# A new order list for a fused linear-attention and gated feed-forward kernel

## The chip, the cores and the metric

The kernel runs on one core of one Trainium2 chip. The metric is the time of one execution in microseconds of the device (us); lower is better. A core has five engines that run side by side, each with its own queue of instructions that it takes strictly in the order written: TensorE (PE, matrix products; its weight loads are listed as PEld), VectorE (DVE), ScalarE (ACT), GpSimd (POOL) and SyncE (SP). An instruction waits for the semaphores of what it needs, and whatever stands behind it on the same engine waits with it. PE reads operands from the on-chip memory SBUF and writes sums to PSUM, which has eight banks here named 0 to 7. Copies between the chip's main memory and SBUF are made by 16 DMA engines; SP and POOL issue them. What POOL issues is listed as the software queue q0 (these loads also turn float32 into bfloat16), what SP issues as the hardware queue q1.

## What is computed

```python
def _attn_ref(q, k, v):                       # 4 batches, 8 heads, 768 positions, 64 per head
    gamma = 1.0 - 2.0 ** (-5.0 - np.arange(H))
    for t in range(S):
        state = gamma * state + np.einsum('bhd,bhe->bhde', k[:, :, t], v[:, :, t])
        y[:, :, t] = scale * np.einsum('bhd,bhde->bhe', q[:, :, t], state)
...
def _moe_ref(x, w_gate, w_val, w_out, rms_g): # x: 3072 rows of 512; 1536 hidden
    xn = x / np.sqrt(np.mean(x * x, axis=-1, keepdims=True) + 1e-06) * rms_g
    g = xn @ w_gate
    return g * (1.0 / (1.0 + np.exp(-g))) * (xn @ w_val) @ w_out
```

A decaying state per head is read by q, its result is normalised row by row, and a gated feed-forward layer follows.

## The kernel before

The 768 positions are cut into six chunks of 128, c = 0 to 5, and each chunk is worked for the four batches b = 0 to 3. The whole program is one string, `ORDER`: a list of some 1060 words. A loop at the end of the kernel takes word after word and calls the small function of that name, which issues its instructions at once. So the list sets the order of every engine's queue; nothing reorders it later. A word reads `name.arguments`, with `@D`, `@A`, `@P` or `@S` for the engine where there is a choice (DVE, ACT, POOL, SP) and `/n` for the PSUM banks. The words that matter here:

- `Lq`, `Lk`, `Lv` .c.b load q, k or v of a chunk and batch (L327, L329). On POOL they arrive as bfloat16; on SP they arrive as float32 in the tiles qf, kf and vf, and `Cq`, `Ck` and `V` turn them into the bfloat16 operands later. `tq` and `tk` are transposing DMAs on SP (L402), and `XE` on SP is another (L516).
- `wg`, `wv` and `wo` .n0.n1 load the weights' column groups n0 to n1 on POOL (L338, L345): w_gate and w_val have twelve groups of 128, loaded in five pieces each, w_out three pieces.
- `Tq`, `Tk` transpose q and k on PE (L381, L386); `A` is the q-k product of one chunk, for one or two batches (L418), with 64 rows of the array used by each matmul; `M0`, `M1` mask it; `Y` forms the result of a chunk (L456, L460).
- `K` is the state product k times v (L541): eight matmuls that each use 64 columns of the array. `U` adds it to the running state and `B` makes the bfloat16 copy that the next chunk's `Y` reads. `P` is `A` and a part of `Y` for two batches together.
- `S`, `R`, `N`, `X`/`XE` are the row normalisation, its reciprocal root on POOL and the transposed copy xnT.
- `g` and `v` .c.n0.n1.b0.b1 are the two products of the feed-forward layer into PSUM (L564), `s` is the activation and `h` the product hT. The last chunk's are done with seven products in place of eight (`ga1` to `vc3`, L750, with sums `gS`, `vS`, `X1` to `X4` of operands).
- `a1`, `a6`, `a7`, `a4`, `b2`, `c5`, `c3` .c.r0.r1 are the seven products of hT and w_out that replace eight (L660), over sums `z1` to `z4` and `w1` to `w4`; `q` keeps a partial sum, `r1` to `r4` form the four quarters of a chunk's result and `s1` to `s4` .c store them (L688). A fourth argument of `a4`, `c3`, `r` and `s` means one half of a quarter.
- `H` and `hot` are matmuls on ones that nobody reads.

A DMA issued from SP uses one of eight completion slots in turn (DMAHW0 to 7), and one from POOL another eight (DMASW0 to 7); the ninth waits until the first has landed. One more rule stands in the load function:

```python
        if c == 2:
            after(i, ("wo", 8))
```

so that the loads of chunk 2 wait until the w_out piece `wo.8.12` has landed. Loads of other chunks have no such line; they wait only for a free buffer (four each of qf and kf, six of vf), for their completion slot, and for what stands ahead of them on their engine.

Of the kernel before, what the change touches and what calls it, by code (L numbers as in the profile page):

```python
# [17 lines left out]
Lk.0.2@S H.8/0 Lk.1.1@S rms.1@S yt ident iota pick Lk.0.0@P Ck.0.2@D Lq.0.1@P Tk.0.2/1 vd Lq.0.0@P mk1 H.3/2 D.0.2@D  # L18
Lk.0.1@P mk0 Lq.0.2@P Lk.0.3@P Lq.0.3@P Tk.0.0/3 Lv.0.0@P H.1/4 Ek.0.0@D Tq.0.1/5 hot.3/6 Lv.0.1@P J.0.0/7 Eq.0.1@A
Tq.0.0/0 D.0.0@D Lv.0.2@P Eq.0.0@A Tk.0.1/2 Ek.0.2@D H.1/4 Ek.0.1@A Tq.0.2/3 Lv.0.3@P yd hot.2/6 A.0.0/5710 Eq.0.2@D  # L20
tab wg.0.2 G/4 M0.0.0 wv.0.2 M1.0.0 Tq.0.3/2 GE@A wg.2.4 M0.0.1 Tk.0.3/6 Eq.0.3@A Y.0.0/3 M1.0.1 Lq.1.1@P A.0.2/57
Ek.0.3@A H.3/4 M1.0.2 S.0.0 A.0.3/12 M0.0.2 R.0.0 H.1/0 M1.0.3 Y.0.2/6 wv.2.4 K.0.0/4 N.0.0 S.0.2 J.0.1/7 Y.0.1/0
H.1/5 M0.0.3 R.0.2 S.0.1 X.0.0/2 J.0.3/3 U.0.0@A XE.0.0@D H.2/5 R.0.1 Ck.1.1@A N.0.2 Y.0.3/1 g.0.0.2.0.1/4 B.0.0 S.0.3
N.0.1 K.0.2/2 X.0.2/5 s.0.0.2.0.1 wg.4.6 v.0.0.2.0.1/6 U.0.2@A XE.0.2@D X.0.1/4 D.0.1@D R.0.3 v.0.0.2.2.3/0 XE.0.1@A
h.0.0.2.0.1 g.0.0.2.2.3/2 wv.4.6 D.0.3@D g.0.0.2.1.2/5 s.0.0.2.2.3 g.0.2.3.0.3/7 causal h.0.0.2.2.3 s.0.0.2.1.2
Lk.1.2@P N.0.3 g.0.3.4.0.3/6 D.1.1@D v.0.0.2.1.2/4 Lk.1.0@P s.0.3.4.0.3 K.0.1/3 s.0.2.3.0.3 h.0.0.2.1.2 X.0.3/2
Tk.1.1/5 mc.0@P U.0.1@A XE.0.3@A Lk.1.3@P g.0.0.4.3.4/0 g.0.4.6.3.4/1 wg.9.12 s.0.0.4.3.4 J.0.2/6 K.0.3/4 Lq.1.2@P
v.0.0.4.3.4/7 Lq.1.3@P v.0.4.6.3.4/3 h.0.0.4.3.4 v.0.2.3.0.3/2 mc.1@P s.0.4.6.3.4 v.0.3.4.0.3/0 U.0.3@A h.0.2.3.0.3
Tk.1.2/6 h.0.4.6.3.4 Lq.1.0@P g.0.5.6.0.3/7 Ek.1.2@D h.0.3.4.0.3 Tq.1.1/1 wv.9.12 s.0.5.6.0.3 g.0.4.5.0.3/4 Eq.1.1@D
wg.6.9 v.0.4.5.0.3/2 Ek.1.1@D s.0.4.5.0.3 Tk.1.0/3 Lv.1.3@P v.0.5.6.0.3/6 Ek.1.0@A g.0.9.10.0.4/0 Lv.1.0@P h.0.5.6.0.3  # L30
h.0.4.5.0.3 Tq.1.3/7 s.0.9.10.0.4 Tk.1.3/1 Lv.1.1@P Eq.1.3@D Tq.1.2/5 Ek.1.3@A Tq.1.0/4 Eq.1.2@D g.0.11.12.0.4/3
Lv.1.2@P Eq.1.0@D A.1.3/62 D.1.0@P s.0.11.12.0.4 g.0.10.11.0.4/0 M0.1.3 M1.1.3 A.1.2/71 wv.6.9 s.0.10.11.0.4
# [12 lines left out]
Cq.2.1@D g.1.2.3.0.3/6 w4@D tk.2.2 B.1.0 g.1.7.8.0.4/7 s.1.2.3.0.3 h.1.9.10.0.4 g.1.10.11.0.4/4 tq.2.3 h.1.2.3.0.3
s.1.4.5.0.4 v.1.5.6.0.4/0 z3.0.2@D z1.1.0@P s.1.7.8.0.4 h.1.4.5.0.4 tk.2.1 v.1.10.11.0.4/6 Cq.2.0@D s.1.10.11.0.4
z3.1.0@P h.1.5.6.0.4 a1.0.0.3/2 Lv.2.2@S h.1.10.11.0.4 tk.2.0 z2.0.2@P v.1.7.8.0.4/5 q1.0@A tq.2.0 V.2.3@A z4.0.2@P
A.2.2/1734 h.1.7.8.0.4 b2.0.0.3/0 M0.2.3 tq.2.1 z1.1.1@P M1.2.3 a6.0.0.3 V.2.0@P M1.2.2 Lv.2.1@S r1.0 Lk.3.3@S V.2.2@P
M0.2.2 Y.2.3/6 Lv.3.3@S q6.0@D S.2.3 A.2.0/5347 Lq.3.1@S R.2.3 a1.1.0.3/0 M0.2.1 M0.2.0 V.2.1@P Lq.3.3@S Y.2.2/1
M1.2.0 a7.0.0.3 z2.1.1@P S.2.2 M1.2.1 N.2.3 Lk.3.2@S R.2.2 Y.2.0/4 z1.1.2@D q7.0@A Y.2.1/5 S.2.0 N.2.2 XE.2.3@S  # L50
K.2.1/3 c5.0.0.3/7 S.2.1 R.2.0 U.2.1@D XE.2.2@S R.2.1 N.2.0 K.2.0/6 a4.0.0.3 z2.1.0@P N.2.1 XE.2.0@S r2.0 K.2.3/1
r4.0@A b2.1.0.3/3 U.2.0@D XE.2.1@S z2.1.2@D q1.1@A U.2.3@D z4.1.2@P Ck.3.3@A z3.1.2@D c3.0.0.3 Lq.3.2@S z4.1.0@P
Lq.3.0@S V.3.3@D K.2.2/4 Lk.3.0@S a6.1.0.3 U.2.2@D B.2.3 r3.0 Lv.3.2@S B.2.1 K.3.3/5 g.2.10.11.0.4/6 Cq.3.3@P U.3.3@D
r1.1 g.2.4.5.0.4/2 s.2.10.11.0.4 Cq.3.1@P tq.3.3 Ck.3.2@A v.2.4.5.0.4/1 s.2.4.5.0.4 B.2.0 tk.3.2 g.2.11.12.0.4/4
h.2.4.5.0.4 B.2.2 z3.1.1@D g.2.5.6.0.4/7 tk.3.3 Cq.3.2@D g.2.2.3.0.4/5 tq.3.2 v.2.10.11.0.4/3 s.2.2.3.0.4 s.2.5.6.0.4
v.2.5.6.0.4/6 Lk.3.1@S h.2.10.11.0.4 Lv.3.1@S Cq.3.0@D v.2.2.3.0.4/2 s.2.11.12.0.4 tq.3.1 Ck.3.0@D g.2.6.7.0.4/1
# [762 lines left out]
```

## Time and profile before

| what | value |
|---|---|
| time, median of 3 runs (lowest to highest) | 230.48 us (230.33 to 231.29) |
| span of the profiled execution, first to last instruction | 228.9 us |
| PE busy | 219.0 us, 96% of the span |
| DVE busy | 179.8 us, 79% |
| POOL busy | 162.5 us, 71% |
| ACT busy | 98.1 us, 43% |
| granted TensorE clock | full in all 40 slices |
| DMA moved | 33.64 MB, mean 147 GB/s |

The runs' times and the profiled execution's span differ by 1.58 us at the median, which lies outside the first and last instruction; the profile gives no other time of its own. The page cuts the span into 40 slices of 5.7 us and gives a busy digit in tenths for each. A group's row gives line, engine, operation and tiles, how many, busy time and mean. The timeline gives start, length and operation; matmuls overlap, so the distance from one start to the next is what a group took, not its length.

### The profile page before, as it was taken

What the parts mean: (1) busy time and instruction counts of PE and PEld (TensorE: products, weight loads), DVE (VectorE), ACT (ScalarE), POOL (GpSimd) and SP (SyncE); (2) the same over time, 40 slices, a digit from 0 to 9 for tenths busy, and PEclk for the clock granted to TensorE, in tenths of its full rate; (3) what the DMA queues carried; (4) which work ended last, traced back from release to release, by engine and by line L of the source; (5) the groups of instructions that cost most, each with busy time, mean ns of one, the idle gap of its engine ahead of it and who ended that gap; (6) DMA issues with size and microseconds to landing.
All of it is one profiled execution on the core that took longest, in us unless ns stands there. A gap on an engine that the chain in (4) does not pass through costs nothing.

```text
span 228.9 us, 5499 instructions
## 1 busy us (share of the span) xinstructions
PE 219.0 (96%) x2119; PEld 145.6 (64%) x2119; DVE 179.8 (79%) x325; ACT 98.1 (43%) x218; POOL 162.5 (71%) x214
## 2 busy tenths in 40 slices
PE   7799989999999999999999999999999999999991
PEld 2568744675447886446574448674457788888871
DVE  6599359889999968679747878791997789999850
ACT  7776342533247252362602424514335328754311
POOL 8979999658998979514584997886198899330800
PEclk9999999999999999999999999999999999999999
DMA  7999999999456888777989579469974432000254
GB/s 134 162 183 131 143 169 177 205 199 241 109 117 138 195 155 171 127 164 172 194 206 204 122 135 259 93 150 226 195 157 157 77 102 92 3 0 3 76 186 153
DMA packets 108171, 33.64 MB, mean 147 GB/s; under 512 B 94449, under 2 KB 108145, under 8 KB 108146
## 3 DMA queue, kind: packets, MB, share of 16 engines
q1 hardware_dynamic: 84674, 25.70, 49.8%
q0 software_dynamic: 23472, 7.60, 30.6%
q8 instruction: 16, 0.26, 0.4%
q14 instruction: 9, 0.07, 0.2%
HBM read 28.31 MB, written 6.29 MB: 151 GB/s over the span
## 4 chain that ended last, share of the span: by engine, by line
PE 59%; ACT 0%; DVE 0%; issue 0%
PE g_ps L564 14%; PE v_ps L564 14%; PE a L660 10%; PE c L660 6%; PE b L660 2%; PE ga L750 2%; PE va L750 2%; PE a_ps L418 1%; PE vc L750 1%; PE gc L750 1%; PE y_ps L456 1%; PE y_ps L460 1%; PE kv_ps L541 1%; PE vb L750 1%; PE gb L750 1%; ACT r L152 0%
## 5 line engine op out<-in xcount | busy, mean ns | idle before, releaser
L574 ACT ACTIVATE sg<-g_ps 128x512 bf16<-128x512 f32 (+2 forms) x64 | 35.9, 570 | 71.1 <-PE g_ps L564 63.2
L564 PE MATMUL g_ps<-xnT,wg_b 128*128 128x512 bf16 (+2 forms) x296 | 58.7, 339 | 0.9 <-ACT xnT L152 0.5
L564 PE MATMUL v_ps<-xnT,wv_b 128*128 128x512 bf16 (+2 forms) x296 | 59.2, 339 | 0.0
L586 DVE TENSOR_TENSOR hT<-sg,v_ps 128x512 bf16<-128x512 bf16 (+2 forms) x64 | 40.1, 647 | 18.7 <-PE v_ps L564 17.5
L564 PEld LDWEIGHTS <-wg_b 128*128 128x128 bf16 x296 | 25.3, 98 | 23.4 <-DMA wg_b<-in_moe_w_gate_dram 0.8
L564 PEld LDWEIGHTS <-wv_b 128*128 128x128 bf16 x296 | 25.6, 98 | 22.3
L660 PEld LDWEIGHTS <-hT 128*128 128x128 bf16 x288 | 27.6, 98 | 4.7
L633 POOL TENSOR_TENSOR z<-hT,z 128x512 bf16<-128x512 bf16 x14 | 16.9, 1218 | 12.7 <-PE a L660 6.7
L660 PEld LDWEIGHTS <-z 128*128 128x128 bf16 x216 | 20.8, 98 | 3.6 <-issue 0.7
L497 DVE SCALAR_TENSOR_TENSOR xn<-y_ps,rstd,g_bc 128x512 bf16<-128x512 f32 x22 | 16.5, 749 | 6.7 <-POOL rstd L485 6.5
L556 POOL CAST st_b<-st_f 64x256 bf16<-64x256 f32 x40 | 20.5, 513 | 1.4
L441 DVE TENSOR_TENSOR am<-a_ps,causal 128x512 bf16<-128x512 f32 x32 | 20.1, 680 | 1.6 <-PE a_ps L418 1.4
L473 ACT ACTIVATE xsq<-y_ps 128x512 bf16<-128x512 f32 x22 | 13.2, 600 | 16.1 <-PE y_ps L460 11.8
L660 PE MATMUL a<-wo_b,hT 128*128 128x256 bf16 x144 | 17.9, 273 | 0.0
L633 POOL TENSOR_TENSOR z<-z,hT 128x512 bf16<-128x512 bf16 x8 | 10.2, 1273 | 7.4 <-DVE z L633 3.8
L485 POOL TENSOR_TENSOR rstd<-ms,mhalf 128x1 f32<-128x1 f32 x24 | 13.7, 570 | 2.0
L483 POOL TENSOR_SCALAR ms<-ssq 128x1 f32<-128x1 f32 x24 | 4.7, 197 | 11.5 <-ACT xsq L473 10.3
L633 POOL TENSOR_TENSOR z<-hT 128x512 bf16<-128x512 bf16 x9 | 10.7, 1190 | 3.0 <-DVE hT L586 2.9
L683 DVE TENSOR_TENSOR r<-c,sn 128x512 f32<-128x512 f32 (+1 forms) x13 | 8.4, 645 | 5.5 <-PE c L660 4.4
L152 ACT COPY sn<-a 128x512 f32<-128x512 f32 x14 | 8.2, 583 | 10.5 <-PE a L660 10.5
L373 POOL TENSOR_TENSOR vp<-vf,vdec 128x512 bf16<-128x512 f32 x11 | 11.5, 1058 | 0.7 <-DMA vf<-in_v_dram 0.7
L441 DVE TENSOR_TENSOR am<-a_ps,mask 128x512 bf16<-128x512 f32 x16 | 10.1, 683 | 0.2 <-PE a_ps L418 0.2
(158 smaller groups left out, 396.0 us busy)
## 6 DMA issues: line engine op xcount, KB each, us to landing
out_dram<-r SPq DMA_DIRECT2D x22, 256.0 KB, 2.4
kf<-in_k_dram SPq DMA_DIRECT2D x18, 256.0 KB, 4.1
qf<-in_q_dram SPq DMA_DIRECT2D x16, 256.0 KB, 3.9
vf<-in_v_dram SPq DMA_DIRECT2D x16, 256.0 KB, 3.7
wo_b<-in_moe_w_out_dram POOLq DMA_DIRECT2D x3, 512.0 KB, 10.0
qb<-in_q_dram POOLq DMA_DIRECT2D x8, 128.0 KB, 5.6
vp<-in_v_dram POOLq DMA_DIRECT2D x8, 128.0 KB, 7.3
kb<-in_k_dram POOLq DMA_DIRECT2D x6, 128.0 KB, 5.1
```

Source lines behind the costliest of these rows:

```text
L373: e.tensor_tensor(out=u["vp"], in0=u["vf"], in1=vdec[:, c, :, None].to_broadcast([128, H, D]), op=ALU.mult)
L441: DVE.tensor_tensor(out=u["am"][:, i], in0=u["a"][i], in1=m, op=ALU.mult)
L473: ACT.activation(xsq, flat(u["y"]), AF.Square, accum_out=u["ssq"])
L485: POOL.tensor_tensor(out=u["rstd"], in0=ms, in1=mhalf, op=ALU.pow)
L497: DVE.scalar_tensor_tensor(out=u["xn"], in0=flat(u["y"]), scalar=u["rstd"], in1=g_bc, op0=ALU.mult, op1=ALU.mult)
L556: POOL.tensor_copy(st_b[b][r, :, i * 64:i * 64 + 64], st_f[b][r])
L564: nc.tensor.matmul(p[:, (n - n0) * m:(n - n0 + 1) * m], W[w][0][:, s, n * 128:(n + 1) * 128], xnT[c][:, s, b0 * C:b1 * C], start=s == 0, s ...
L574: ACT.activation(sg[:, :cols], done["wg", c, n0, b0][:, :cols], AF.Silu)
L586: DVE.tensor_tensor(out=h_of(c, r)[:, i:i + n1 - n0, b0 * C:b1 * C], in0=sg, in1=p, op=ALU.mult)
L633: e.tensor_tensor(out=x, in0=a, in1=b, op=how)
L660: nc.tensor.matmul(done[x, c][:, q], left(i, c, r)[:, k, q * C:q * C + C], right(i)[:, r, k], start=first and q == r == k == 0, stop=r == ...
L750: nc.tensor.matmul(p[:, q], l[:, r, q], m[:, k], start=first and q == k == 0, stop=q == k == 1, skip_group_check=True)
```

## The change

The change is a new string `ORDER`; no other line differs. The same operations are called as before, except that the words `a4.4.0.3`, `r4.4` and `s4.4` (the last quarter of chunk 4) are each split into two halves. Some elementwise operations are given to another engine (about ninety words change their letter, as many towards DVE as away from it), and the banks differ. On PE the state products `K` now stand next to each other or next to an `A`: counted along PE's queue, the 41 groups of `A`, `K`, `P` and of transposes onto half the array stood in 39 separate places before and stand in 22 now. Of the weights, `wv.2.4` is now issued before `wg.2.4` and `wg.4.6` before the first load of chunk 1 on POOL; `wo.8.12` now stands ahead of `wg.6.9` and `wv.6.9`. The word `yd` (an exponential on ACT) moves behind the first activations.

```diff
-Lk.0.2@S H.8/0 Lk.1.1@S rms.1@S yt ident iota pick Lk.0.0@P Ck.0.2@D Lq.0.1@P Tk.0.2/1 vd Lq.0.0@P mk1 H.3/2 D.0.2@D
...
+H.1/0 rms.1@S Lq.0.2@P H.3/1 Lk.0.0@P Lk.0.2@S Lq.0.0@P yt Lk.0.1@P Lq.0.1@P H.2/2 iota H.8/3 H.3/4 H.1/5 Lk.0.3@P
...
```

The head of SP's queue before, with what each row waits for (kf, qf and vf are loads of k, q and v):

```order
L329 DMA kf<-in_k_dram 128x8x64 x2
L306 DMA g_row<-in_moe_rms_g_dram 1x512
L329 DMA qf<-in_q_dram 128x8x64 [waits DMASW1_49]
L329 DMA kf<-in_k_dram 128x8x64 x2
L329 DMA qf<-in_q_dram 128x8x64
```

and now, up to the first load of chunk 2, the row that waits for DMASW4:

```order
L306 DMA g_row<-in_moe_rms_g_dram 1x512
L329 DMA kf<-in_k_dram 128x8x64 x2
L329 DMA qf<-in_q_dram 128x8x64
L329 DMA vf<-in_v_dram 128x8x64 x3
L329 DMA kf<-in_k_dram 128x8x64
L329 DMA qf<-in_q_dram 128x8x64 [waits DMAHW0_49]
L329 DMA kf<-in_k_dram 128x8x64 [waits DMAHW1_49]
L329 DMA kf<-in_k_dram 128x8x64 [waits DMAHW2_49,Activation_49]
L329 DMA qf<-in_q_dram 128x8x64 [waits DMAHW3_49]
L329 DMA vf<-in_v_dram 128x8x64 [waits DMAHW4_49]
L402 DMA_TRANSPOSE kT<-kb 128x4x128 [waits DVE_49,DMAHW5_49,PE_49,Activation_49]
L329 DMA kf<-in_k_dram 128x8x64 [waits DMAHW6_49,DVE_49]
L329 DMA kf<-in_k_dram 128x8x64 [waits DMAHW1_49,DMAHW7_49,DMASW4_49,DVE_49]
```

Before, two loads were issued and then came a load of chunk 2 (the qf row that waits for DMASW1, the slot of `wo.8.12`). Now twelve loads stand ahead of the first transpose, ten of them of chunks 3 and 4.

POOL's queue before, from the piece `wv.9.12` on:

```order
L338 DMA wv_b<-in_moe_w_val_dram 128x4x384
L338 DMA wg_b<-in_moe_w_gate_dram 128x4x384
L329 DMA vp<-in_v_dram 128x8x64 x4
L532 TENSOR_TENSOR kd<-kb,vdec 128x512
L338 DMA wv_b<-in_moe_w_val_dram 128x4x384
L345 DMA wo_b<-in_moe_w_out_dram 128x4x512
```

and now, from the same piece:

```order
L338 DMA wv_b<-in_moe_w_val_dram 128x4x384
L297 TENSOR_TENSOR mask_102<-causal,vdec 128x512
L345 DMA wo_b<-in_moe_w_out_dram 128x4x512
L556 CAST st_b_128<-st_f_124 64x4x64 x2
L556 CAST st_b_126<-st_f_122 64x4x64 x2
L329 DMA vp<-in_v_dram 128x8x64
L338 DMA wg_b<-in_moe_w_gate_dram 128x4x384
L338 DMA wv_b<-in_moe_w_val_dram 128x4x384
```

The last two of the twelve column groups' pieces, `wg.6.9` and `wv.6.9`, now come behind a piece of w_out of 512 KB, which is `wo.8.12`.

PE's queue in chunk 2 before, one row for each new product (kv_ps is a state product, and each row stands for the matmuls of its product):

```order
L541 MATMUL kv_ps_1678<-vp_1597,kb_1353 64x64
L660 MATMUL c_1687<-w1_1254,z_985 128x256
L541 MATMUL kv_ps_1715<-vp_1521,kb_1348 64x64
L660 MATMUL a_1428<-w4_1380,hT_588 128x256
L541 MATMUL kv_ps_1743<-vp_1457,kb_1307 64x64
L660 MATMUL b_1754<-wo_b_135,hT_1246 128x256
```

and now:

```order
L660 MATMUL a_1488<-wo_b_135,hT_627 128x256
L541 MATMUL kv_ps_1665<-vp_1278,kb_1303 64x64
L541 MATMUL kv_ps_1694<-vp_1376,kb_1301 64x64
L541 MATMUL kv_ps_1711<-vp_1625,kb_1238 64x64
L541 MATMUL kv_ps_1730<-vp_1550,kb_1188 64x64
L564 MATMUL v_ps_1739<-xnT_1041,wv_b_134 128x512
```

The four state products of a chunk, each between two full-array products before, now follow one another.

More of the change, by code (lines that the diff above doesn't have):

```diff
@@ L23 @@
[L23 to L32, printed above, removed]
@@ L103 @@
-c3.5.2.3.1 r3.5.1 c3.5.2.3.0 r3.5.0 s4.5.1@S s4.5.0@S s3.5.0@S s3.5.1@S b2.5.2.3 r1.5 s1.5@S z4.4.1@P c3.4.0.3 r3.4
-s3.4@S a4.4.0.3 r4.4@A s4.4@S
+H.1/0 rms.1@S Lq.0.2@P H.3/1 Lk.0.0@P Lk.0.2@S Lq.0.0@P yt Lk.0.1@P Lq.0.1@P H.2/2 iota H.8/3 H.3/4 H.1/5 Lk.0.3@P
+ident mk0 H.1/6 Lv.0.2@P H.1/7 Lv.0.0@P Ck.0.2@A G/0 Tk.0.2/1 pick Tq.0.2/2 Ek.0.2@D vd D.0.2@D Lq.0.3@P Tk.0.0/3 mk1
+Eq.0.2@A causal A.0.2/45 Lv.0.1@P Ek.0.0@D Tq.0.0/6 Eq.0.0@A Tk.0.1/7 Ek.0.1@A wg.0.2 Lv.0.3@P J.0.0/1 Tq.0.1/2 tab
```

158 lines of the change are left out of this document (84 added, 74 removed).

## The prediction

> **What bounds the kernel now.** I read the page first, then the waits of PE, the chain of waits, the timeline of the start, and last the DMA's rates by stretch. On the page:
>
> ```profile
> span 228.9 us, 5499 instructions
> PE 219.0 (96%) x2119; PEld 145.6 (64%) x2119; DVE 179.8 (79%) x325; ACT 98.1 (43%) x218; POOL 162.5 (71%) x214
> PE   7799989999999999999999999999999999999991
> DMA  7999999999456888777989579469974432000254
> ```
>
> PE is busy in all but the ends. In the first ten slices, up to 57 us, the DMA engines are as full as PE. The waits of PE, those of the first 90 us and then the one late wait:
>
> ```profile
> PE t_ps L381 <- DMA kb<-in_k_dram: 1.3, 1, 1.3
> PE g_ps L564 <- DMA wg_b<-in_moe_w_gate_dram: 0.4, 1, 0.4
> PE kv_ps L541 <- DVE vp L373: 0.4, 1, 0.4
> ...
> PE c L660 <- DVE r L683: 0.5, 1, 0.5
> ```
>
> So from about 35 us on PE runs through, with 0.9 us of waits, and the end is set by when PE gets its last weights and by its work from there. Up to that point the loads pace it: the wait of 0.4 us is for a weight piece. I therefore count from the first use of the last piece of w_val, `wv.6.9`, by the word `v.0.8.9`; about the same PE work stands ahead of it in both orders. Its issue on POOL, the time such a piece takes to land, and its first use on PE:
>
> ```profile
> 35.36 0.82 POOL L338 DMA_DIRECT2D wv_b<-in_moe_w_val_dram  x1
> ...
> wv_b<-in_moe_w_val_dram POOLq DMA_DIRECT2D x2, 384.0 KB, 7.5
> ...
> 45.22 1.03 PE L564 MATMUL v_ps<-xnT,wv_b 128*128 128x512 bf16 x4
> ```
>
> It lands at about 35.36 + 7.5 = 42.9 and is used at 45.22: the order has 2.3 us to spare there, no more.
>
> **Loads on SP: the term that decides.** Before, SP issues two loads of k at the start and then stands still:
>
> ```profile
> 0.79 1.06 SPq L329 DMA_DIRECT2D kf<-in_k_dram  x2
> ...
> SPq L329 <- DMA wo_b<-in_moe_w_out_dram: 46.1, 1, 46.1
> ```
>
> It waits 46.1 us for `wo.8.12`, because the next row is a load of chunk 2. In the new order ten loads of chunks 3 and 4 stand ahead of that row. The first seven loads wait for nothing and the next five for landings of early ones and for one cast on ACT. So the chip issues them in the first microseconds, wherever the list has them, and they meet the loads that PE needs. The DMA's rate by stretch (the last three columns are the granted clock, the mean share of a DMA engine and GB/s):
>
> ```profile
> 3.40:3.90 0.50, 0.50 (x3) 0.15 (x1) 0.50 (x3) 0.50 (x3) 0.50 (x2) 1.00 1.24 281
> 3.80:48.80 45.00, 41.82 (x582) 27.01 (x580) 33.81 (x59) 25.04 (x62) 39.46 (x62) 1.00 1.55 170
> 41.00:48.00 7.00, 7.00 (x83) 4.21 (x80) 5.80 (x10) 4.72 (x12) 4.47 (x10) 1.00 1.25 206
> 50.50:58.50 8.00, 8.00 (x65) 4.42 (x62) 7.73 (x13) 2.56 (x5) 6.83 (x7) 1.00 1.08 245
> ```
>
> From 3.8 to 48.8 only POOL's queue moves data, and the engines' share stays above one: packets queue up all that time. From 50.5 to 58.5 only SP's loads move, at 245 GB/s and a share of 1.08, which is full too. At 3.4 to 3.9 both queues are at work, and the share (1.24) is no higher than for one alone (1.25 in 41 to 48). The two queues divide one capacity. A load on SP is 262,144 bytes: 1.07 us at 245 GB/s, 0.93 us at 281. Ten of them take 9.3 to 10.7 us of all 16 engines. The price for the piece `wv.6.9` lies between 0, if POOL's queue were served first, and 10.7 us, if all ten are through before it. I take 9.3, from the row in which both queues run. It needs no even division: what SP's queue is given in the first 45 us is lost to POOL's, and at a quarter of the engines all ten would be through by then. At one seventh, the 40 us of POOL's loads from 3.8 to the landing of `wv.6.9` would still take 40 x 7/6 = 46.7, 6.7 us more.
>
> On this the Trainium skill, DMA: Bandwidth & Descriptors, section "Queues, rings and completion order", says that a DMA engine goes round the queue rows that have work and drains one packet from each in turn. By that rule SP's loads get their turns from the start, and the sum stays as it is; the trace has only the half microsecond of 3.4 to 3.9 with both at work.
>
> Behind these loads on SP stand transposes and the loads of chunk 2; on POOL, the reciprocal roots of chunk 0's normalisation stand behind weight loads that wait for one of eight slots to land. Both come late by the same wait for data, so I don't count them again.
>
> **Order of the weights.** `wo.8.12`, 512 KB, now stands ahead of `wv.6.9`, so its landing moves by 524,288 bytes at 206 GB/s, 2.5 us, to 45.4. Without any crowding `v.0.8.9` would start at about 45.5, 0.3 us later than before; the slack covers the rest. The pieces issued sooner are early ones, and what sets the later pace is the last. `wo.8.12` is also the gate of chunk 2: when it has landed, up to five loads of chunk 2 join `wg.6.9` and `wv.6.9` on the engines, which costs from 0 to 5 x 1.07 = 5.4 us. Before SP comes to them it has a transpose that waits for a cast, and most of `wg.6.9` is moved by then; I take 0.5.
>
> **State products side by side.** The price of a change between full-array products and half-array ones, from the chain (start, length, what):
>
> ```profile
> 105.27 0.24 PE kv_ps L541 x8
> 105.52 1.42 PE a L660 x12
> ...
> 116.67 1.31 PE a L660 x12
> ```
>
> and from the timeline of the start, two transposes onto half the array that follow one another:
>
> ```profile
> 11.80 0.44 PE L381 MATMUL t_ps<-pick,qb 128*64 128x64 bf16 x16
> 12.07 0.42 PE L381 MATMUL t_ps<-pick,kb 128*64 128x64 bf16 x16
> ```
>
> A state product of eight matmuls takes 0.24 us, and makes the product behind it 0.11 longer (1.42 against 1.31): 0.35. Sixteen such matmuls among their like take 0.27 (11.80 to 12.07), eight 0.135. The change of mode costs 0.21 us, there and back. The places of half-array work fall from 39 to 22; behind `v.0.8.9` from 23 to 11. Twelve fewer are 2.5 us. All of this is on PE's own path, with no cover; the five ahead of `v.0.8.9` save nothing, since PE waits for loads there. The bounds are 0 and 3.6 us (all 17).
>
> The skill's page TensorEngine Tiling (Array Packing), section "Key Properties", says that changing the mode drains the array while changing only the tile does not. By it, the two merges of a state product with a q-k product save only half each, 0.2 us less in all; no row here has such a pair.
>
> **The end.** The last rows on the way out, and the landing of stores of 256 and 128 KB:
>
> ```profile
> 220.35 0.42 DVE L683 TENSOR_TENSOR r<-c,sn 128x256 f32<-128x256 f32 x1 [1.38 <-PE c L660]
> ...
> 224.30 0.58 ACT L152 COPY r<-a 128x512 f32<-128x512 f32 x1 [3.80 <-PE a L660]
> ...
> out_dram<-r SPq DMA_DIRECT2D x22, 256.0 KB, 2.4
> ...
> out_dram<-r SPq DMA_DIRECT2D x4, 128.0 KB, 1.7
> ```
>
> PE ends at 224.27 (before the row at 224.30), and 4.63 us follow. The last piece is now half a quarter: 0.42 in place of 0.58, and 1.7 in place of 2.4, so 0.85 less, 3.8. The other half of chunk 4's quarter lies between the halves of `c3.5`, which covers the wait of 0.5 us for DVE's r. The stores before it could still be under way: 0 to 0.85.
>
> **Other moves.** `yd` behind the activations brings two more table loads on ACT:
>
> ```profile
> L302 ACT ACT_TABLE_LOAD x1 | 1.3, 1283 | 0.0
> ```
>
> Twice 1.28 us, while ACT is 43% busy, and behind it wait an activation and a copy of chunk 0's xnT. The late weights hide it; uncovered it could cost up to 2.6. Some ninety elementwise words change engine. DVE and POOL at 79% and 71% have room, but a single word can come late: the rows of 0.4 and 0.5 us above are such cases. I drop those two waits (0.9) and put 0.5 in, with 0 to 1.5 as bounds.
>
> **The sum**, against the profiled execution: `v.0.8.9` at 45.5 + 9.3 + 0.5 = 55.3. From there to PE's end before: 224.27 - 45.22 = 179.05; less 2.5, less 0.9, plus 0.5 is 176.15. PE ends at 231.45; plus 3.8 is a span of 235.25. The runs lie 1.58 above the span (230.48 against 228.9): **236.8 us**.
>
> **The rivals.**
> - *No crowding: faster.* POOL's queue keeps its rate and SP's loads fill gaps. Then 45.5 + 176.15 + 3.8 + 1.58 = **227.0 us**. For it: the mean of 170 GB/s against 206 leaves some gaps, and the two queues overlap for half a microsecond only. Against it: a share above one through 45 us. It decides if SP's ten loads cost POOL's queue under 2.5 us.
> - *Half the crowding: no change.* If SP's loads get a tenth of the engines or finish partly in gaps, 4 to 5 us are lost, and the savings of 3.5 to 4 us cancel them: 227.0 + 4.5 = **231.5**.
> - *Both crowdings: slower still.* The loads of chunk 2 go ahead of `wg.6.9` and `wv.6.9` too: 236.8 + 4.9 = **241.7**. For it: these are the last pieces, with 2.3 us to spare before. Against it: the transpose ahead of them on SP.
> - *The savings fail.* Neighbouring state products cost as before: 236.8 + 2.5 = 239.3, inside the forecast's range.
>
> **Chances.** The forecast with its own range, 233 to 240: 0.62. No crowding 0.20, half of it 0.08, both 0.10. Differences under 0.5% (1.15 us) can't be told from no change in this kernel. Faster by more: 0.20; within: 0.05; slower: 0.75, which has the rest of the half case. For eight in ten the range goes from 226.5 to 241.
>
> **What would show it.** Right: on SP twelve loads issued within the first 15 us; POOL's landings late by some 9 us at 45; PE idle before 57 us, on loads of q, k, v and weights, for about 10 us more than before; `v.0.8.9` near 55; from there on the same chain, shorter by 2.5 us; four state products of chunk 2 in about 0.65 us plus 0.1. Wrong: if the weights land as before and PE starts `v.0.8.9` before 47, the crowding is not there. If PE waits late for DVE or POOL by more than 1.5 us, the exchange of engines matters more than I said.

## The result and the profile after

| | before | after |
|---|---|---|
| time, median (lowest to highest) | 230.78 us (230.33 to 231.29) | 262.44 us (261.31 to 262.76) |
| ratio with 95% interval | | 1.1388 (1.1329 to 1.1448) |
| span of the profiled execution | 228.9 us | 259.6 us |

The change costs 31.7 us; the forecast was 6.3, and its whole range, up to 241, lies below the result. The page of the changed kernel, with its row of the clock:

```profile
PE 225.8 (87%) x2097; PEld 150.1 (58%) x2119; DVE 188.5 (73%) x324; ACT 96.6 (37%) x204; POOL 163.9 (63%) x218
...
PE   8837759976179799999989999999999979999894
...
PEclk9977988999759979999999999999999999999999
```

PE falls to a tenth of a slice where slices were full before, and the clock, which was full throughout, drops there and just behind to as little as a half. The DMA's rows by queue from 4 to 47 us (packets, MB, share of 16 engines), before:

```profile
q0 software_dynamic: 22946, 7.09, 155.6%
...
q1 hardware_dynamic: 179, 0.04, 0.5%
```

and after:

```profile
q0 software_dynamic: 18465, 4.76, 109.8%
q1 hardware_dynamic: 11439, 2.88, 46.6%
```

The sum hardly moves (7.13 and 7.64 MB). Of the 2.88 MB that SP's queue got, POOL's queue lost 2.33. SP's timeline after, and then PE, POOL and ACT around the forecast's mark:

```profile
2.29 0.99 SPq L329 DMA_DIRECT2D qf<-in_q_dram  x1
3.32 6.65 SPq L329 DMA_DIRECT2D vf<-in_v_dram  x3
...
27.21 4.02 SPq L329 DMA_DIRECT2D vf<-in_v_dram  x1
45.87 1.29 SPq L402 DMA_TRANSPOSE kT<-kb  x1
47.26 6.08 SPq L329 DMA_DIRECT2D kf<-in_k_dram  x3
```

```profile
62.40 1.04 PE L564 MATMUL v_ps<-xnT,wv_b 128*128 128x512 bf16 x4 [1.79 <-DMA wv_b<-in_moe_w_val_dram]
...
69.83 0.42 PE L541 MATMUL kv_ps<-vp,kd 128*64 128x64 bf16 x8 [4.08 <-ACT sg L574]
...
72.58 0.61 PE L510 MATMUL xt_ps<-ident,xn 128*128 128x128 bf16 x4 [2.32 <-DVE xn L497]
```

```profile
69.78 1.03 POOL L354 TENSOR_TENSOR qb<-qf,ydec 128x512 bf16<-128x512 f32 x1 [10.86 <-DMA qf<-in_q_dram]
70.90 0.19 POOL L483 TENSOR_SCALAR ms<-ssq 128x1 f32<-128x1 f32 x1
```

```profile
68.67 0.62 ACT L152 CAST kb<-kf 128x512 bf16<-128x512 f32 x1 [6.50 <-DMA kf<-in_k_dram]
```

`v.0.8.9` starts at 62.40 in place of 45.22. Behind it POOL stands 10.86 us on the cast `Cq.2.3`, whose load of q has not landed, with the reciprocal root `R.1.1` queued behind. ACT stands 6.50 us on the cast `Ck.2.0`, with an activation behind. PE waits 4.08 us for that activation and 2.32 for the xn that the root releases, and runs at half clock there (from 68 to 77 us). In the list before, `Cq.2.3` had 19 us of PE work between `v.0.8.9` and itself; in the new one it has 0.9. The waits of PE from 110 us on are these; all but the second lie behind 190 us, in the new end, and sum to 3.4:

```profile
PE a L660 <- DVE hT L633: 1.8, 1, 1.8
PE y_ps L460 <- POOL st_b L556: 0.9, 1, 0.9
PE a L660 <- DVE sn L152: 0.7, 1, 0.7
PE a L660 <- DVE vf L762: 0.4, 1, 0.4
PE a L660 <- ACT sn L152: 0.3, 1, 0.3
PE vb L750 <- DVE vf L762: 0.2, 1, 0.2
```

Before, there was one wait of 0.5 in all that time. Two of the forecast's small terms hold. The four state products of chunk 2 take 0.63 us from start to start, and the last rows on PE end at 256.05, 3.55 us before the span's end:

```profile
106.24 0.69 PE L541 MATMUL kv_ps<-vp,kb 128*64 128x64 bf16 x32
106.87 1.04 PE L564 MATMUL v_ps<-xnT,wv_b 128*128 128x512 bf16 x3
...
255.67 0.38 PE L660 MATMUL c<-wo_b,z 128*128 128x256 bf16 x2
```

### The profile page after: what moved, and what is told of

It reads as the page before. It is cut to its first block, busy times and chain, and to the rows that moved or that the text cites. A ratio compares the mean times of both kernels' runs of the same rounds, so it can differ in the third digit from the quotient of the medians.

```text
span 259.6 us, 5453 instructions
## 1 busy us (share of the span) xinstructions
PE 225.8 (87%) x2097; PEld 150.1 (58%) x2119; DVE 188.5 (73%) x324; ACT 96.6 (37%) x204; POOL 163.9 (63%) x218
## 3 DMA queue, kind: packets, MB, share of 16 engines
q1 hardware_dynamic: 84690, 25.70, 46.2%
## 4 chain that ended last, share of the span: by engine, by line
PE 38%; DVE 8%; POOL 7%; DMA 4%; issue 1%; SPq 1%; ACT 0%; POOLq 0%; DVEq 0%
PE v_ps L564 9%; PE g_ps L564 9%; PE a L660 8%; PE c L660 4%; DMA qf<-in_q_dram 4%; DVE hT L586 4%; DVE vf L762 2%; POOL vp L373 2%; POOL z L633 2%; PE b L660 2%; POOL st_b L556 1%; PE ga L750 1%; PE y_ps L460 1%; PE va L750 1%; PE y_ps L456 1%
## 5 line engine op out<-in xcount | busy, mean ns | idle before, releaser
L564 PE MATMUL v_ps<-xnT,wv_b 128*128 128x512 bf16 (+2 forms) x284 | 63.3, 355 | 6.5 <-DMA wv_b<-in_moe_w_val_dram 3.6
L564 PE MATMUL g_ps<-xnT,wg_b 128*128 128x512 bf16 (+2 forms) x286 | 61.0, 348 | 1.9 <-DMA wg_b<-in_moe_w_gate_dram 1.1
L586 DVE TENSOR_TENSOR hT<-sg,v_ps 128x512 bf16<-128x512 bf16 (+2 forms) x64 | 40.4, 646 | 20.3 <-ACT sg L574 11.9
L564 PEld LDWEIGHTS <-wv_b 128*128 128x128 bf16 x296 | 27.2, 103 | 30.0 <-issue 5.8
L564 PEld LDWEIGHTS <-wg_b 128*128 128x128 bf16 x296 | 27.0, 102 | 24.3 <-issue 2.0
L633 POOL TENSOR_TENSOR z<-hT 128x512 bf16<-128x512 bf16 x12 | 14.4, 1201 | 16.0 <-DVE hT L586 15.8
L354 POOL TENSOR_TENSOR qb<-qf,ydec 128x512 bf16<-128x512 f32 x9 | 10.2, 1132 | 18.5 <-DMA qf<-in_q_dram 17.6
L633 POOL TENSOR_TENSOR z<-hT,z 128x512 bf16<-128x512 bf16 x11 | 14.6, 1331 | 4.7 <-DVE z L633 4.4
L373 POOL TENSOR_TENSOR vp<-vf,vdec 128x512 bf16<-128x512 f32 x13 | 13.8, 1069 | 0.2
L633 POOL TENSOR_TENSOR z<-z,hT 128x512 bf16<-128x512 bf16 x11 | 13.0, 1185 | 0.8 <-DVE z L633 0.6
L456 PE MATMUL y_ps<-vp,am 128*128 128x64 bf16 x176 | 8.9, 195 | 4.6 <-DMA vp<-in_v_dram 4.5
```

The source lines that it names most:

```text
L373: e.tensor_tensor(out=u["vp"], in0=u["vf"], in1=vdec[:, c, :, None].to_broadcast([128, H, D]), op=ALU.mult)
L456: nc.tensor.matmul(y[:, h, :], u["am"][:, h % 2, h // 2, :], u["vp"][:, h, :], start=h == 0, stop=c == 0 and h == H - 1, skip_group_check= ...
L564: nc.tensor.matmul(p[:, (n - n0) * m:(n - n0 + 1) * m], W[w][0][:, s, n * 128:(n + 1) * 128], xnT[c][:, s, b0 * C:b1 * C], start=s == 0, s ...
L586: DVE.tensor_tensor(out=h_of(c, r)[:, i:i + n1 - n0, b0 * C:b1 * C], in0=sg, in1=p, op=ALU.mult)
L633: e.tensor_tensor(out=x, in0=a, in1=b, op=how)
```

## The experiments

### Early loads alone, in the order before

Ten and five extra loads on SP, with nothing else changed:

```diff
+    def early(e, bk, n):
+        for i in range(n):
+            x = ring([128, H, D], F32, *(("qf", 4) if i < 4 else ("vf", 6)))
+            SP.dma_start(out=x, in_=rows["k"][i % B, 3 + i // B])
...
-rms.1@S yt
+rms.1@S early.10 yt
```

> The order before, with ten more loads on SP's queue behind its first three: 256 KB each, k of chunks 3 to 5, into the four qf and the six vf buffers that are free at the start. Nobody reads them; they are extra work, and the rest of the computation is untouched. SP's own later loads come behind them as before, with the same gate. First theory (SP's loads take the DMA engines from POOL's loads, and what waits for POOL's loads is late): POOL's queue moves about 4.8 MB between 4 and 47 us in place of 7.1, v.0.8.9 starts at 57 to 62 us in place of 45.2, PE has waits for loads and some of the clock is lost behind them; 243 to 255 us. Rival theory (the new order of the work on PE, DVE and POOL costs the time and early loads are harmless): within 2 us of before, 229 to 233. The forecast's own size for the crowding (9.3 us) would give 240.

> The same with five extra loads, into the four qf buffers and one vf buffer, read by nobody. First theory: the loss goes with the bytes that SP's queue moves in the first 45 us, so about half of that with ten: v.0.8.9 at 50 to 53 us, 236 to 243 us. If even five loads have slack to fill, 230 to 233, and the loss has a threshold. Rival theory: 229 to 232, as with ten.

Measured, in one execution each: 242.04 us with ten and 237.46 with five, against 230.16 before: 11.9 and 7.3 us. The first lies 1 us under the first theory's range, the second inside it; the rival is out. PE's first use of the last w_val piece, with ten and then with five:

```profile
56.79 1.03 PE L570 MATMUL v_ps<-xnT,wv_b 128*128 128x512 bf16 x4
```

```profile
51.61 1.03 PE L570 MATMUL v_ps<-xnT,wv_b 128*128 128x512 bf16 x4
```

It comes 11.6 and 6.4 us late, and nearly all the loss is there: behind it PE has the same two small waits as before (0.4 and 0.5). With ten loads POOL's queue moved 5.03 MB from 4 to 47 us. So the crowding is real in an order that is otherwise untouched, and five loads already pay it. A load costs 1.2 to 1.5 us, more than the 0.93 to 1.07 that the forecast worked out for its bytes. But these loads explain 12 of the 31.7 us.

### The early loads taken out of the new order

```diff
-M0.0.3 Lq.3.2@S J.0.3/6
+M0.0.3 J.0.3/6
...
-Lv.2.2@S tq.3.2 Ck.3.1@P
+Lv.2.2@S Lq.3.2@S Lk.3.2@S Lk.3.3@S Lq.3.3@S Lk.3.1@S Lv.3.0@S Lv.3.2@S Ck.3.1@P
```

> The new order, with the early loads of chunks 3 and 4 on SP, and the words that convert them, moved behind the loads of chunk 2, which still wait for wo.8.12. All other words stand as in the new order; nothing is left out. First theory: POOL's queue gets the engines back (about 7 MB between 4 and 47 us), v.0.8.9 starts at 45 to 50 us, the clock stays full, and the time is 226 to 233 us. Rival theory: the time stays above 245, since the order of the other work is unchanged.

Measured: 255.22 us, ratio 1.1076 (1.0992 to 1.1159). Both theories missed. POOL's queue has its rate back (6.58 MB) and `v.0.8.9` starts in time, but then (PE, then POOL):

```profile
47.34 1.03 PE L565 MATMUL v_ps<-xnT,wv_b 128*128 128x512 bf16 x4
...
56.88 0.61 PE L511 MATMUL xt_ps<-ident,xn 128*128 128x128 bf16 x4 [3.90 <-DVE xn L498]
```

```profile
54.09 1.03 POOL L355 TENSOR_TENSOR qb<-qf,ydec 128x512 bf16<-128x512 f32 x1 [6.55 <-DMA qf<-in_q_dram]
```

Fifteen microseconds are won by 47 us, and half of them is lost again by 90, since the casts of chunk 2 now wait in an order in which nothing else is late. My edit added a wait of its own: POOL stands 10.7 us, until 72.3, on a cast of chunk 3, which kept its place while its load had moved back.

### One cast ahead of its data

First `Cq.2.3` moved behind the root in the new order, then the reverse, the same cast moved ahead of the root in the order before, and its load to the first place behind the gate:

```diff
-v.0.8.9.0.4/7 Cq.2.3@P tq.2.3 N.1.0
+v.0.8.9.0.4/7 N.1.0
...
-R.1.1 Ck.2.0@A
+R.1.1 Cq.2.3@P tq.2.3 Ck.2.0@A
```

> The new order, with the cast Cq.2.3 on POOL (and the transposing DMA tq.2.3 that reads it) moved behind the reciprocal root R.1.1. In the new order that cast waits for a late load of q until 69.8 us with the root behind it, and PE waits 4.1 and 2.3 us behind ACT and DVE just there, with the clock at half for the next ten microseconds. If the cast's wait is what holds PE: PE's waits between 62 and 75 us fall from some 6.4 us to under 3, less half clock, and 255 to 259 us. If the wait only moves (to the next word on POOL, or PE is held by the loads of chunk 2 in the end anyway): 261 to 263.

```diff
-v.0.7.8.0.4/5 R.1.1
+v.0.7.8.0.4/5 Lq.2.3@S Cq.2.3@P R.1.1
```

> The order before, with one thing of the new one: the cast Cq.2.3 on POOL stands directly ahead of the reciprocal root R.1.1 (in the order before it stands some fifteen words behind it), and its load Lq.2.3 is the first on SP behind the gate. Nothing else moves. If a cast ahead of its data is a cause: POOL waits from about 47 until the load has landed at 51 to 53 us, N.1.1 and X.1.1 behind it, and PE, which takes X.1.1 at 49.7 before, idles 3 to 5 us there and loses another 1 to 2 by the clock: 233 to 237 us. Rival: PE has other work to do and the engines catch up: 230 to 231.5.

Measured, in one execution each: 258.52 us for the first, 3.9 less than the changed kernel, and 237.9 for the second, 7.7 more than before and 0.9 above the range expected. In the first, PE no longer waits for xn (2.32 in the changed kernel), and for the activation 2.9 us in place of 4.08; what is left stands behind ACT's own cast of k. The second, on POOL, on PE, and by windows (the third figure from the end is the granted clock):

```profile
53.64 1.04 POOL L354 TENSOR_TENSOR qb<-qf,ydec 128x512 bf16<-128x512 f32 x1 [5.43 <-DMA qf<-in_q_dram]
```

```profile
56.43 0.61 PE L510 MATMUL xt_ps<-ident,xn 128*128 128x128 bf16 x4 [5.54 <-DVE xn L497]
```

```profile
53.00:56.40 3.40, 0.00 (x0) 0.00 (x0) 0.78 (x2) 0.00 (x0) 1.78 (x3) 0.96 1.07 238
56.40:60.00 3.60, 3.52 (x31) 2.68 (x33) 3.33 (x8) 0.00 (x0) 1.82 (x2) 0.57 1.11 252
60.00:63.00 3.00, 3.00 (x24) 1.54 (x23) 3.00 (x5) 1.57 (x3) 2.51 (x3) 1.00 0.28 63
```

PE idles 5.54 us, then works 3.6 us at 0.57 of its clock, which is another 1.5 (3.6 x 0.43). The last microsecond stood already in the weights of this execution (`v.0.8.9` at 46.22). So one cast, moved ahead by some fifteen instructions of POOL's queue, or 18 us of PE work, costs about 7 us, a fifth of what the whole change costs.

### Old places for the loads and casts

Every load, cast and transposing DMA of chunks 2 to 4, or of chunk 2 alone, put back to its old place among the new products; the lists differ in some hundred words, of which these show the kind:

```diff
-v.0.8.9.0.4/7 Cq.2.3@P tq.2.3 N.1.0
+v.0.8.9.0.4/7 N.1.0
...
-v.1.5.6.0.4/2 v.1.6.7.0.4/1
+v.1.5.6.0.4/2 Cq.2.3@P v.1.6.7.0.4/1
```

> The new order, but with every load, conversion and transposing DMA of chunks 2 to 4 put back to the place that it has in the order before (counted by how much PE work stands ahead of it), on the engine that it had there. So no loads ahead of the gate, and chunk 2's casts stand behind the normalisation of chunk 1. PE's products, the state products side by side, the weights' order and the tail stay new; nothing is left out. Theory now: two separate losses, the early loads and the casts of chunk 2 that hold POOL, DVE and ACT before their data is there; with both gone PE waits under 3 us behind 47 us, the clock stays full from there, and the time is 226 to 231 us, the forecast's sum without crowding (227.0). Rival: something else in the new order of PE's, DVE's and POOL's work loses as well; then 235 to 255, with PE waiting for DVE and ACT between 50 and 90 us.

> The new order with only chunk 2's loads, conversions and transposing DMAs put back to their old places; the early loads of chunks 3 and 4 stay ahead of the gate. If the two losses are separate and add, this keeps the loss of the early loads alone: 237 to 243 us, v.0.8.9 at 57 to 63, few PE waits behind that. If most of the loss came through chunk 2's casts in any case (late data for them): 230 to 236. If the early loads hurt more in the new order than in the old: above 245.

Measured: 268.3 us (ratio 1.1653, 1.1599 to 1.1707) and 264.78 (one execution), slower than the change. The theory fell: the old places are too late for the new products. `A.2.2` stands about 19 us of PE work behind `v.0.8.9` now, about 26 before, and in the first of these two kernels PE waits for its operands there and again in chunk 3 (waits of PE: us in total, times, the longest):

```profile
PE a_ps L418 <- DMA qT<-qb: 11.2, 5, 4.8
PE y_ps L456 <- POOL vp L373: 5.1, 2, 2.8
PE a_ps L418 <- DMA kT<-kb: 4.0, 2, 3.3
```

### Casts put by hand where their data should have landed

Three versions, each mending the waits that the one before had shown: chunk 2 and 3, then chunk 4 as well, then v. Some of the places, of the first (two), the second and the third:

```diff
-v.0.8.9.0.4/7 Cq.2.3@P tq.2.3 N.1.0
+v.0.8.9.0.4/7 N.1.0
...
-g.1.1.2.0.3/6 Lk.2.3@S Lk.2.1@S V.2.1@P z2.0.2@D
+g.1.1.2.0.3/6 Cq.2.3@P z2.0.2@D
...
-z3.1.0@D Ck.4.1@A s.2.2.3.0.4
+z3.1.0@D s.2.2.3.0.4
...
-A.3.2/6214 V.5.0@P M0.3.2
+A.3.2/6214 M0.3.2
```

> The new order, with chunk 2's ten loads in a row right behind the gate, its transposing DMAs behind them, each of its casts moved back to where its load should have landed (1 to 14 us of PE work later), and all loads, casts and transposing DMAs of chunk 3 and the early ones of chunks 4 and 5 behind chunk 2's. PE's products, the weights and the tail stand as in the new order; nothing is left out. Theory: the early loads and the casts ahead of their data are the two causes; with both gone v.0.8.9 starts at 46 to 49 us, PE waits under 5 us from there to the last product besides the 3.4 us that every kernel with the new end shows, and the time is 228 to 236. Rival: PE's products of chunks 2 and 3 come sooner in the new order (A.2.2 stands 19 us of PE work behind v.0.8.9, 26 before), so that their data can't be there whatever the casts' places: PE waits 5 us and more on a_ps, and 240 to 255.

> The new order with chunk 2's loads and casts moved as in the run before, and now also those of chunks 3 and 4: the transposing DMAs of chunk 3 directly behind its casts, and the casts of chunk 4 (Ck.4.1 on ACT and Cq.4.0 on POOL above all, which waited 13.8 and 11.1 us there) 12 us of PE work later, behind their loads. PE's products, the weights and the tail stand as in the new order; nothing is left out. Theory: what was left there was again casts ahead of their data; without the 11.6 and 4.9 us of PE's waits and some 3 us of half clock behind them, 259.8 becomes 237 to 242, PE waits no more than 3 us at a time, and v.0.8.9 starts at 47 to 48.5. Rival: the waits move to another place, and the time stays above 248.

> The run before, with the rest of the late data put right: the loads of v of chunk 3 ahead of those of chunks 4 and 5, the conversions of v (chunks 2 to 5) on POOL later, and the transposing DMAs of xnT of chunk 2 on SP ahead of those of q and k of chunk 3. Nothing is left out. Theory: the waits of 5.3 us (vp) and 5.5 us (st_b behind the same conversions), the 2.6 us on xnT and the half clock behind them go, some 13 to 16 us: 236 to 241 us, of which 3.4 us are the waits in the new order's end. If the new order's products then had the gain that the forecast gave them, it would be below 230. Rival: the waits move on again, 245 and above.

Measured: 259.8, 252.41 and 253.59 us. `v.0.8.9` starts at 47.80, 46.21 and 47.45, and from there on the largest wait moves on, each time to the next word that is ahead of its data. In the first version it is ACT, and PE waits 11.6 us behind it:

```profile
112.05 0.62 ACT L153 CAST kb<-kf 128x512 bf16<-128x512 f32 x1 [13.76 <-DMA kf<-in_k_dram]
```

In the second it is POOL's conversions of v (5.3 and 5.5 us of PE), in the third a cast of chunk 5 on DVE, which stands 7.40 us on its load until 129.84 (4.9 us of PE).

The waits moved on each time, as the rivals said; the first version came out above even its rival's range. The second and the third differ by no more than their executions do. I did not find places by hand that suit the new products.

One run with the third version and the ten extra loads told nothing of what it was for:

> The same kernel with the ten early loads of the first experiment added on SP (256 KB each, read by nobody, extra work). If early loads cost in the new order what they cost in the old one, it is 11 to 13 us slower than the run without them, with v.0.8.9 at 56 to 60 us. If they cost more (17 us, as v.0.8.9 was late in the changed kernel): 16 to 19 us slower. If less, because the new order has other work to do meanwhile: under 8.

Measured, in one execution: 277.27 us. The extra loads stood ahead of SP's load of k of chunk 1, and PE waited 25.2 us for that one alone.

### The order without the loads

Chunks 2 to 5 are not loaded, in both kernels (48 loads are left out and the casts read a tile that is there); then all loads are there, and only the casts read something else. The results are not the reference's in any of them:

```diff
+        elif c >= 2:
+            t[c, b][n + "f"] = t[0, 2]["kf"]
+            return
...
+            if c >= 2:
+                t[c, b][n + "f"] = g_bc.rearrange("p (h d) -> p h d", h=H)
```

> The changed kernel without any load of q, k and v of chunks 2 to 5: their casts read, in place of the loaded tiles, the tile of k of chunk 0 and batch 2 that SP loads at the start. So 48 loads of 256 KB are left out and the values are not the reference's; every other instruction, its engine and its place stay. Theory: the new order of the work itself is sound and the loss is all loads, by crowding and by casts that wait for them. Then 223 to 230 us, v.0.8.9 at 44 to 48 us and PE's waits behind it only the 3.4 us in the new end. Rival: the exchange of engines and places on PE, DVE and POOL loses by itself; then above 238.

> The kernel before without the same 48 loads, for comparison. Its PE waits only 0.9 us behind 35 us and none of it for those loads, so 228.5 to 230.5 us; below 227 if even the loads behind the gate slow POOL's weights or the stores. The difference between the two kernels without loads is what the new order of the work is worth by itself: by the forecast's steps 2.5 (joints) and 0.85 (tail) less, against some 3 us of new waits in the end, so between 3 us faster and 1 us slower.

> The changed kernel with all its loads issued as they are, but the casts of chunks 2 to 5 read another tile, the broadcast row g that is there from the start, in place of the loaded tiles. So the values are not the reference's, the DMA traffic stays, and no cast waits for a load any more. Against the kernel without loads (237.4) it prices the traffic alone, and the changed kernel (262.4) against it prices the casts' waits. If the traffic costs what v.0.8.9 was late (17 us), 252 to 256 us, with 6 to 10 us left for the casts; if it costs what ten early loads cost in the old order (11.9), 247 to 251, with 11 to 15 for the casts; if the traffic alone is nearly all, above 258.

Measured: 237.44 us for the new order without loads, 231.36 for the old one without them, and 256.08 for the new one with free casts. With free casts the queues move what they move in the changed kernel (4.70 and 2.88 MB from 4 to 47 us, there 4.76 and 2.88), so the traffic is the same. This divides the loss, by medians:

| step | us | difference |
|---|---|---|
| old order, no loads of chunks 2 to 5 | 231.36 | |
| new order, no loads of chunks 2 to 5 | 237.44 | 6.1: the order of the work itself |
| new order, loads as traffic, casts free | 256.08 | 18.6: traffic |
| new order as it is | 262.44 | 6.4: casts that wait |

The old order is no slower with its loads than without (230.22 beside 231.36 in the same series). Neither forecast for the pair held: I had the new order between 3 us faster and 1 slower. The chief waits of PE in the new order without those loads, some left out:

```profile
PE a_ps L421 <- ACT qT L152: 2.3, 2, 1.9
PE a_ps L421 <- DVE hT L589: 2.0, 1, 2.0
PE a L663 <- DVE hT L636: 1.7, 1, 1.7
```

They are products that come right behind the elementwise word they need: a copy of qT on ACT at 14 us, products hT at 71, a sum of hT near 200. With free casts, the rows of 4.08 and 2.32 us are gone from PE's waits. That their sum is the 6.4 of the table is in part luck: waits for DVE of 1.4, 1.3 and 0.8 us have come, and others have shrunk. What stays is the late piece:

```profile
64.34 1.89 PE L566 MATMUL v_ps<-xnT,wv_b 128*128 128x512 bf16 x4 [2.06 <-DMA wv_b<-in_moe_w_val_dram]
```

That is 15.9 us behind the 48.47 of the same kernel without loads; 11.6 of it is what ten loads cost in the order before, and 4.3 comes on top while chunk 2's first loads (issued from 49 us here, from 47 in the changed kernel) run beside `wg.6.9` and `wv.6.9`. In the changed kernel itself, with the piece used at 62.40, the same difference is 2.4.

Last, both at once: the early loads moved back and the casts free.

> Both at once: the early loads of chunks 3 and 4 moved behind chunk 2's loads, and the casts of chunks 2 to 5 reading the row g in place of the loaded tiles (so the values are not the reference's; all loads are still issued). The fourth corner of a square: neither undone 262.4, early loads moved 255.2, casts freed 256.1. If the two losses simply add, 248 to 250. If one hides in the other (while the weights are late the casts' waits are covered in part, and with the weights in time the casts' waits come to the front), this run falls further than the sum, to what the order takes without loads, 237 to 241.

Measured: 250.96 us in three of the four executions (250.14 to 251.9), ratio 1.0945 (1.0871 to 1.102). It is 2 us above the plain sum (249) and far from 237, so the two don't hide in each other. The profiled execution is the fourth, of 253.91, so I read only its largest wait:

```profile
PE a_ps L421 <- DMA kT<-kb: 7.0, 2, 6.8
```

That is a wait of the kind which the old places showed: the transposing DMA of chunk 2 against a product that comes 7 us of PE work sooner than before. In the changed kernel it was covered, as PE itself was 17 us late there. So with both causes undone 13.5 us (250.96 - 237.44) are still lost to the loads in their other places, and the 18.6 of the table are not what one gets back by moving the early ones.

### The credit side, in the order before

> The order before, with only the tail of the new one: the words a4.4.0.3, r4.4 and s4.4 each in two halves, with c3.4 between them. By the forecast's step the copy is 0.42 in place of 0.58 us and the last store 1.7 in place of 2.4: 0.85 us less, 229.3 to 229.9. If the stores ahead of it are still under way then, 230.0 to 230.5, no difference that can be told.

Measured: 229.38 us, ratio 0.9967 (0.9946 to 0.9988), 0.8 us less. The step holds.

```diff
-c3.4.0.3 r3.4 s3.4@S a4.4.0.3 r4.4@A s4.4@S
+a4.4.0.3.0 r4.4.0@A s4.4.0@S c3.4.0.3 r3.4 s3.4@S a4.4.0.3.1 r4.4.1@A s4.4.1@S
```

For the joints of state products:

```diff
-K.2.1/3 c5.0.0.3/7 S.2.1
+c5.0.0.3/7 K.2.1/3 K.2.0/6 K.2.3/1 S.2.1
...
-K.4.3/3 s.3.4.5.0.4 g.3.6.7.0.4/0
+K.4.3/3 K.4.1/5 s.3.4.5.0.4 g.3.6.7.0.4/0
```

> The order before, with eleven state products of chunks 2 to 4 brought next to each other in six joints (K.2.1, K.2.0 and K.2.3; K.2.2 and K.3.3; K.3.1 and K.3.0; K.4.3 and K.4.1; K.4.0 and K.4.2), by moving seven words a little. Nothing else. By the forecast's step each joint saves 0.21 us: 1.26 us, 228.9 to 229.3. If the change of mode costs nothing here, or a wait for a bank or a cast takes it back: 230.0 to 230.7.

> The order before with the six joints of state products and the halved tail, the two things of the new order that the forecast put on the credit side. Both hold and add: 1.26 + 0.8 us less, 228.0 to 228.6. If only the tail holds: 229.2 to 229.7.

Measured: 229.63 us, ratio 0.9987 (0.9958 to 1.0015) for the joints, not to be told from no change; 228.98 us, 0.9943 (0.9912 to 0.9973), for both. Neither reached what was expected (228.9 to 229.3, and 228.0 to 228.6). On PE the joint of K.4.3 and K.4.1, from start to start, before and then with the edit:

```profile
130.79 0.32 PE L541 MATMUL kv_ps<-vp,kb 128*64 128x64 bf16 x8
131.04 1.04 PE L564 MATMUL g_ps<-xnT,wg_b 128*128 128x512 bf16 x4
132.01 0.32 PE L541 MATMUL kv_ps<-vp,kb 128*64 128x64 bf16 x8
132.25 1.04 PE L564 MATMUL v_ps<-xnT,wv_b 128*128 128x512 bf16 x4
```

```profile
130.05 0.44 PE L541 MATMUL kv_ps<-vp,kb 128*64 128x64 bf16 x16
130.42 1.04 PE L564 MATMUL g_ps<-xnT,wg_b 128*128 128x512 bf16 x4
131.30 1.03 PE L564 MATMUL v_ps<-xnT,wv_b 128*128 128x512 bf16 x4
```

Apart, the two state products take 0.25 and 0.24, and the product between them, with a state product on both its sides, 0.97 (131.04 to 132.01). Together they take 0.37, and the product behind them, with a state product on one side, 0.88 (130.42 to 131.30). So a joint saves 0.12 + 0.09 = 0.21, which is the forecast's 0.21. But in chunk 2 one of the products brought together waits 0.48 us for a PSUM bank that a normalisation still reads, more than its two joints save; another waits 0.3 for its vp, as it did before (0.4). The kernel with the tail and the joints is faster than both kernels here, by 1.3 us (0.6 to 2.0) against the one before.

## Why the prediction was wrong

The direction was right, the size wrong by 25.6 us. Step by step, in the profiled execution:

- **Weights order, `v.0.8.9` at 45.5 without crowding.** It starts at 46.2 to 48.5 in the seven kernels with the new head and no early loads. The step "about the same PE work stands ahead of it" was off: up to there PE is busy for 42.8 us in the new order without loads, and for 40.9 before. PE also waits for ACT's qT (2.3, above), most of it while ACT does a table load of 1.28 us (from 12.43 in the changed kernel), just ahead of that copy. Mis-sized by 1 to 3 us.
- **Crowding, 9.3 with bounds 0 and 10.7.** The mechanism was right, and the term too small: ten loads cost 11.6 us at this mark in the order before, above the upper bound. The bound took the bytes at 245 GB/s, the rate of SP's loads alone. In the changed kernel the two queues together move 178 GB/s (7.64 MB in 43 us), and a 256 KB load costs the other queue 1.2 us and not 0.93.
- **Second crowding, 0.5 with bounds 0 and 5.4.** 2.4 us by difference in the changed kernel, 4.3 with free casts: inside the bounds, far above the 0.5. The transposing DMA that was to hold chunk 2's loads back was through at 47 us, with `wg.6.9` just issued, since the weights themselves were late.
- Together: 62.40 in place of 55.3, 7.1 of the missing microseconds (3.0, 2.3 and 1.9).
- **"Both come late by the same wait for data, so I don't count them again."** This step failed. Lateness doesn't pass through in-order queues once: it adds where a word that waits for its own late load stands ahead of a word that does not. I saw the roots behind the weight loads, and not the casts of chunk 2, five of which the list had brought about 10 to 19 us of PE work closer to `v.0.8.9` (an estimate from the products between, by their rows). From there to PE's end it took 193.65 us, in place of 176.15. Some 13 us of it are waits of PE (9.1 from there to 110 us, 4.3 later), where I had put 0.5 with a bound of 1.5. How the 17.5 us divide is seen from the same stretch in the runs above: without loads it goes from 48.47 to PE's end at 234.07, with free casts from 64.34 to 252.04 (the last rows on PE start at 233.69 and 251.66 and take 0.38). They take 185.60 and 187.70 us. So the step that I put at nothing was worth 8.1 us: 6.0 are casts that wait (193.65 - 187.70), and 2.1 are other loads. The remaining 9.4 (185.60 - 176.15) are not the loads' at all.
- **New waits, 0.5, and the credit.** This step failed too, by those 9.4 us in the profiled executions and about 2 less by the medians, since the one without loads was the longest of its four. Its waits of PE behind `v.0.8.9` sum to 8.1 us, 3.4 of them in the new end, where there were 0.9 before. They are more than twice the credit for joints and tail (3.35). I had counted places on PE and not asked, product by product, how long ago its operand was made.
- **The clock** was not priced at all. In the profiled execution the stretch from 62.4 to 75 us runs at 0.71 and that from 75 to 110 at 0.91:

```profile
62.40:75.00 12.60, 5.98 (x48) 3.12 (x50) 3.83 (x6) 2.66 (x5) 5.05 (x7) 0.71 0.88 172
75.00:110.00 35.00, 32.32 (x261) 18.84 (x264) 31.22 (x46) 12.13 (x26) 25.53 (x30) 0.91 0.77 157
```

  The second alone is worth about 3 us (35 x 0.09), and it lies inside the stretch above.
- **Joints 2.5 and tail 0.85.** Both right in size, on their rows; only the tail also in time. Six joints in the order before were to give 1.26 us and gave 0.3, with an interval that ends at 1.0.

Of the rivals, both crowdings together (241.7) was the mechanism that came, and its price stopped at the weights. What I had named as showing it wrong, PE waiting late for DVE or POOL by more than 1.5 us, is what the profile shows. What stays open is whether any places for the loads, casts and transposing DMAs would suit the new products; six kernels did not find them, and the order without loads, at 237.44, makes it unlikely that even then it would beat the order before.

## What to carry to other kernels

On engines that take their work in order, ask for each moved word that waits for a transfer: when does that transfer land, and what stands behind the word that does not need it; a cast some fifteen places of its queue too early cost about 7 us. Ask the same of each product: how long ago was its operand made? An early load is not free where the DMA engines are full, even if nobody waits for it. And undoing one cause of several gives back little while the next stands right behind it: taking the inputs away (no loads, free casts) priced the parts here where moving them did not.

## What the chip showed that I had not expected

The two queues share nearly evenly. From 4 to 31 us, while both had work, the rows after are:

```profile
q0 software_dynamic: 7930, 2.71, 85.7%
q1 hardware_dynamic: 8895, 2.24, 56.2%
```

The Trainium skill, DMA: Bandwidth & Descriptors, section "Queues, rings and completion order", has each DMA engine take a packet from every queue with work in turn. The counts, 7930 and 8895 packets, are close to even, as this rule would have it if its packets are those of the profile, which no run here shows.

SP's issues take longer while the DMA engines are full. In the rows of SP's timeline above, the issue at 2.29 took 0.99, the next three 2.2 each (6.65 / 3) and the last 4.02, so that the twelve end at 31 us and not within 15, as I had read from the list. From 72 us, with the weights through, one takes 0.5 to 0.6 again.

One idle of PE of 5.5 us cost 3.6 us at 0.57 of the clock (the cast ahead of its root, above). The Trainium skill, TensorE: Matmul & The Clock Gate, section "The HAM clock gate", gives a window of about 3.4 us for going to half and for coming back. The trace agrees with it on the way back: the clock was at half from 56.1 to 59.5, 3.4 us. It had fallen 5.2 us after PE's last matmul. In the changed kernel, with two idles of PE behind one another, it was at half from 67.6 to 77.9.
